# Token rows of 2112 bytes instead of 2056 in a sliding-window attention and expert-routing kernel

## The chip, the core and the metric

The kernel runs on one core of one Trainium2 chip. The metric is the device time of one execution in microseconds (us). TensorE (PE in the profile, PEld for its weight loads) multiplies matrices, VectorE (DVE) and ScalarE (ACT) do elementwise work, GpSimd (POOL) builds constants and issues the indirect transfers, and SyncE (SP) issues the plain transfers between memory and the core's on-chip memory of 128 partitions.

## What is computed

The first half is causal attention over a window of 128 positions, for 8 sequences of 576 tokens with 8 heads of 64 values. The second half is a mixture of experts without dropped tokens: each of the 4608 tokens (rows of 512 values) goes to the one of 8 experts with the largest gate logit.

```python
rel = pos[:, None] - pos[None, :]
scores = scale * q @ k.T - slope[h] * abs(rel)      # where 0 <= rel < 128, else -1e9
x = softmax(scores) @ v                             # (8, 8, 576, 64) -> (4608, 512)
logits = x @ w_gate                                 # 8 experts
e = argmax(logits, axis=1)
y = maximum(x @ w1[e], 0) @ w2[e]                   # 512 -> 1024 -> 512, by expert
out = softmax(logits)[e] * y
```

All values are float32.

## The kernel before, in words

**Attention and routing (about 0 to 226 us).** The work goes in units `u` of one sequence and one pair of heads, 32 in all. In each turn of the loop over `u`, `load_qk` and `load_v` ask SyncE for data some turns ahead, `scores(u)` does 36 small matmuls (L639) whose exponentials ScalarE takes (L646), `values(u - 1)` multiplies by v (L672), and `factors(u)` on VectorE applies the position factors and the mask (L652, L657). When a sequence is complete, its routing is spread over the turns that follow: logits, the chosen expert, and the place of each token in that expert's region of a table in memory (`pick`, `place`, which leave row numbers in `slots`). The order of the instructions on each engine is the order in which this code is written out (`manual_schedule`); no planner moves them.

**The token rows.** The table `x_rows` in memory has one region of 4608 rows for each expert. A row is `RW` values: the 512 values of the token, its number as an integer, and one over the sum of its gate exponentials. With `RW = Dm + 2` that is 514 values, 2056 bytes. `row` writes the 512 values for two tiles of 128 tokens into a buffer `xs` (L807, VectorE). The two trailing values lie ready in a small tile `ends`: the token numbers are put in once (L603), the gate weights by sequence (L791). `send` lets GpSimd copy them behind the row (L820), and `scatter` then issues an indirect transfer of 128 rows from `xs` into `x_rows` (L135). There are 36 such scatters. Slots of a region that hold no token are filled with `zero_row`, also by indirect transfers from L135 (`clear`), whose token number is out of range so that the result is dropped later.

**The hand-over.** Expert 0 has its first 256 rows read early: `early_group` clears what is unused of them, reads them back (L851), and `last_tasks` runs their first layer between the last pieces of routing. SyncE's read of the next rows of expert 0 (L1151) can only be issued when the last scatter and the last clear have landed.

**Experts (226 us on).** For each expert a group of 4 tiles of 128 rows, then a group of one tile for what lies above 512 rows. `gather` reads the group's rows into `xg` (L1151), `turn` transposes them on TensorE (L497), `tokens` copies the two trailing values out (L485, L486), the layers are matmuls of 256 columns in a seven-product scheme (L1048) or plain ones (L506, L517), and `send_out` scatters the results to the output by token number (L465). The weights of the next groups and the rows of the next groups are loaded while a group is computed. SyncE runs its loads in the order of the code, each when its buffer is free.

**On-chip memory.** Tiles are placed one behind the other in pools, each rounded up to 32 bytes per partition. The pools `consts` and `rte` lie first, so a change of size in them moves all tiles behind. `tab` is a pool of the attention stage alone, and its space is used again by the experts. The function `shifted` is a second, slower form of the attention for inputs whose sums leave a safe range; it stands in the program, and none of its lines has an instruction in the trace.

Of the kernel before, what the change touches and what calls it, by code (L numbers as in the profile page):

```python
# [8 lines left out]
F32 = mybir.dt.float32  # L9
# [6 lines left out]
P = 128  # L16
# [5 lines left out]
def kernel(  # L22
# [12 lines left out]
    nc = tc.nc  # L35

    Dm, N = qT.shape
# [3 lines left out]
    NT = N // P  # L41
# [19 lines left out]
    rte = ctx.enter_context(tc.tile_pool(name="rte", bufs=1))  # L61
# [50 lines left out]
    lmin = rte.tile([P, NT], F32, name="lmin")  # L112


    RW = Dm + 2
    x_d = nc.dram_tensor("x_rows", (E * N, RW), F32, kind="Internal").ap()
    zero_row = consts.tile([P, RW], F32, name="zero_row")
    soon.append(lambda: nc.gpsimd.memset(zero_row[:], 0.0))
# [25 lines left out]
    def clear(rows, apart=True):  # L144
        for j in range(rows.shape[1]):
            to_x_rows(zero_row[:], rows[:, j : j + 1], apart)
# [65 lines left out]
    def number_all_free(tmp_pool):  # L212

        tmp = tmp_pool.tile([P, E, NJ], F32, name="free", bufs=1)
        late = tmp_pool.tile([P, 1], F32, name="late", bufs=1)
        nc.vector.tensor_scalar_max(late[:], cnt[:, 0:1], float(EJ * P))
        number_free(
            late_free[:], tmp[:, 0, :EJ], late[:].to_broadcast([P, EJ]), tail[:, :EJ],
            region[:, 0:1].to_broadcast([P, EJ]), CAP,
        )  # L220
        number_free(
            free_rows[:], tmp[:], cnt[:].unsqueeze(2).to_broadcast([P, E, NJ]),
            tail[:, None, :].to_broadcast([P, E, NJ]), region[:].unsqueeze(2).to_broadcast([P, E, NJ]), CAP,
        )

    def scatter(t, row):
        to_x_rows(row, slots[:, t : t + 1])
# [26 lines left out]
    def shifted():  # L254
        with tc.tile_pool(name="bias", bufs=1) as b_pool, \
# [44 lines left out]
            for t in range(NT):  # L300
# [77 lines left out]
                gw = rows.tile([P, 1], F32, name="gw")  # L378
                nc.scalar.activation(gex[:], lgn[:, t, :], AF.Exp, bias=lmin[:, t : t + 1], scale=-1.0, accum_out=gw[:])
                nc.vector.tensor_scalar_add(gw[:], gw[:], 1e-9)  # L380
                if t == NT - 1:
                    number_all_free(rows)
                xs = rows.tile([P, RW], F32, name="xs")
                nc.scalar.copy(xs[:, :Dm], xf)
                nc.vector.tensor_copy(xs.bitcast(I32)[:, Dm : Dm + 1], tok_i[:, t : t + 1])
                nc.vector.reciprocal(xs[:, Dm + 1 :], gw[:])
                scatter(t, xs[:])


# [163 lines left out]
    with tc.tile_pool(name="tab", bufs=1) as tab, \  # L553
# [45 lines left out]
        rs_all = rte.tile([P, NT, H], F32, name="rs_all")  # L599
        gsum = rte.tile([P, NT], F32, name="gsum")  # L600

        ends = rte.tile([P, NT, 2], F32, name="ends")
        later.append(lambda: nc.vector.tensor_copy(ends.bitcast(I32)[:, :, 0], tok_i[:]))  # L603
        q_sb, k_sb, v_sb, xT, lT = {}, {}, {}, {}, {}
        probs, exps, sums = {}, {}, {}
# [190 lines left out]
        def row(ts, i):  # L796
            t = ts[i]
            pair, c = t // TP, t % TP * P
            if i % RG == 0:
                xs_of[t] = rows.tile([P, RG, RW], F32, name="xs", bufs=3)  # L800
            xs = xs_of[t] = xs_of[ts[i // RG * RG]]
# [46 lines left out]
        def early_group():  # L848
            clear(early_free, False)
            g = dict(n=EJ, apart=True, xg=plain.tile([P, EJ, RW], F32, name="xg2"))  # L850
            nc.sync.dma_start(g["xg"][:], x_d[: EJ * P, :].rearrange("(j p) r -> p j r", p=P))  # L851
# [292 lines left out]
    def gather(g):  # L1144
        n = g["n"]
        if g.get("e", 0) > 0:
            clear(free_rows[:, g["e"], :])
        xg = g["xg"] = pools["x"].tile([P, NJ, RW], F32, name="xg")
        src = g["rows"]().rearrange("(j p) r -> p j r", p=P)
# [120 lines left out]
    with nothing.Else():  # L1270
        n_bad = nc.values_load(n_more_i[0:1, 1:2], min_val=0, max_val=N * H)
        with tc.If(n_bad > 0):
            n_pass[0] = 1
            shifted()
            clear(free_rows[:, 0, :])
            with moe_pools(), tc.manual_schedule():
                experts(False)

        n_short = nc.values_load(n_more_i[0:1, 3:4], min_val=0, max_val=EJ * P)
        with tc.If(n_short > 0):  # L1280
            with moe_pools():
                plain_group(dict(n=EJ, e=0, rows=lambda: x_d[: EJ * P, :], apart=False))

        nx = nc.values_load(n_more_i[0:1, 0:1], min_val=0, max_val=NX)
        with tc.If(nx > XU):
            with moe_pools(), tc.For_i(XU, nx, 1) as i:
                mk = pools["u"].tile([P, 2, 1], I32, name="mk")
                nc.vector.tensor_copy(mk[:], xmasks[:, :, bass.ds(i, 1)])
                x = bass.ds(i, 1)
                plain_group(dict(n=1, x=x, rows=lambda: rows_of_x(x), mask=mk, apart=False))  # L1290
# [29 lines left out]
```

## Time and profile before

| what | us |
|---|---|
| three runs | 723.05, 723.74, 725.93 (median 723.74) |
| span of the profiled execution | 722.1 |
| TensorE busy in the span | 689.2 (95%) |
| VectorE, ScalarE, GpSimd busy | 345.5, 215.5, 120.2 |
| moved between memory and core | 121.49 MB, 168 GB/s over the span |
| one indirect transfer of rows on GpSimd | about 1.0, of 107 |

An engine that is busy nearly all the time leaves little to win by anything that other engines or transfers do. So the questions to the profile are where TensorE is idle, what ends each of these idle stretches, and whether one of them hangs on a token row.

### The profile page before, as it was taken

Reading aid. Unit: us, or ns where it says so; the run is one execution under the profiler, and the core shown is the slowest. Engines: PE = TensorE matmul, PEld = TensorE weight load, DVE = VectorE, ACT = ScalarE, POOL = GpSimd, SP = SyncE. Lnnn points to the kernel's source line nnn. Section 1 sums busy time; section 2 is a strip of 40 time slices with the busy share of each in tenths; the row PEclk is TensorE's granted clock in tenths of the full one; section 3 lists DMA queues with packets and bytes.
Section 4 is the critical chain, followed back from the end, with each engine's and each line's share of the span. In section 5 each row is a group of like instructions: output and inputs, shape, how many; then the busy total and the mean of one; then the engine's idle time right before and its main releaser. Section 6 shows DMA issues by size and latency. Waiting matters only on the chain.

```text
span 722.1 us, 13669 instructions
## 1 busy us (share of the span) xinstructions
PE 689.2 (95%) x5662; PEld 560.0 (78%) x5662; DVE 345.5 (48%) x705; ACT 215.5 (30%) x543; POOL 120.2 (17%) x146
## 2 busy tenths in 40 slices
PE   6999999999899999999999999999999999999991
PEld 5777676776676678878897887889788888978880
DVE  4577566575763354326335533634462463435300
ACT  6655454554411121122131212112121221212120
POOL 1010322023443020121022002202200220200020
PEclk9999999899999999999999999999999999999996
DMA  9976799852226726265353617534352835371010
GB/s 275 270 213 188 238 259 296 229 175 75 90 86 215 268 89 232 64 234 175 132 183 141 236 58 284 188 133 161 143 192 115 283 120 201 99 271 53 1 60 4
DMA packets 52722, 121.49 MB, mean 168 GB/s; under 512 B 7185, under 2 KB 7185, under 8 KB 52656
## 3 DMA queue, kind: packets, MB, share of 16 engines
q1 hardware_dynamic: 43568, 101.50, 43.7%
q0 software_dynamic: 8560, 19.06, 7.1%
q8 instruction: 45, 0.74, 0.4%
q14 instruction: 21, 0.17, 0.1%
q10 hardware_dynamic: 528, 0.02, 0.0%
HBM read 101.51 MB, written 28.12 MB: 180 GB/s over the span
## 4 chain that ended last, share of the span: by engine, by line
PE 82%; issue 11%; DVE 3%; POOL 1%; DMA 1%; ACT 0%; SPq 0%; POOLq 0%; DVEq 0%
PE b L1048 17%; PE a L1048 11%; PE c L1048 11%; PE m L672 7%; PE sp L639 7%; PE a L517 6%; PE sm L693 3%; PE b L506 3%; PE a L506 3%; PE m L804 2%; PE m L506 2%; PE c L506 2%; PE tp L497 1%; PE m L753 1%; PE c L517 1%
## 5 line engine op out<-in xcount | busy, mean ns | idle before, releaser
L465 POOL DMA_INDIRECT out_dram<-zo,si x28 | 29.7, 1060 | 292.8 <-ACT zo L1118 288.5
L646 ACT ACTIVATE e<-sp 128x384 f32<-128x384 f32 x128 | 55.8, 491 | 51.8 <-PE sp L639 30.8
L672 PE MATMUL m<-probs,v_sb 64*64 64x192 f32 (+2 forms) x1152 | 64.4, 315 | 6.6 <-issue 4.8
L672 PEld LDWEIGHTS m<-probs,v_sb 64*64 64x64 f32 x1152 | 52.7, 135 | 18.4 <-issue 10.8
L639 PE MATMUL sp<-q_sb,k_sb 64*64 64x192 f32 (+2 forms) x1152 | 57.9, 326 | 7.1 <-DMA k_sb<-in_kT_dram 5.2
L639 PEld LDWEIGHTS sp<-q_sb,k_sb 64*64 64x64 f32 x1152 | 47.5, 139 | 18.4 <-issue 12.9
L517 PE MATMUL a<-w,h 128*128 128x512 f32 x128 | 56.3, 592 | 0.0
L1118 ACT ACTIVATE zo<-zo,gw 128x256 f32<-128x256 f32 x42 | 19.1, 501 | 119.4 <-DVE zo L1129 78.2
L1048 PE MATMUL a<-xgT,w 128*128 128x256 f32 x224 | 53.0, 379 | 0.0
L1048 PE MATMUL b<-xTs,w1s 128*128 128x256 f32 x224 | 52.9, 379 | 0.0
L1048 PE MATMUL a<-w,h_sb 128*128 128x256 f32 x224 | 50.6, 379 | 0.0
L1048 PE MATMUL b<-w2s,hs 128*128 128x256 f32 x224 | 50.6, 379 | 0.0
L1048 PEld LDWEIGHTS a<-xgT,w 128*128 128x128 f32 x224 | 42.5, 190 | 8.7 <-issue 3.3
L1048 PEld LDWEIGHTS b<-xTs,w1s 128*128 128x128 f32 x224 | 42.6, 190 | 5.8
L1048 PEld LDWEIGHTS b<-w2s,hs 128*128 128x128 f32 x224 | 42.6, 190 | 5.8
L1048 PEld LDWEIGHTS a<-w,h_sb 128*128 128x128 f32 x224 | 42.0, 190 | 5.4
L652 DVE TENSOR_TENSOR probs<-e,fac 128x1152 f32<-128x1152 f32 x32 | 43.2, 1351 | 2.8 <-ACT e L646 2.8
L517 PEld LDWEIGHTS a<-w,h 128*128 128x128 f32 x128 | 23.7, 190 | 26.8 <-issue 26.8
L135 POOL DMA_INDIRECT x_rows<-xs,slots x36 | 37.9, 1053 | 15.1 <-POOL xs L820 6.4
L1078 DVE TENSOR_TENSOR u<-b,p 128x512 f32<-128x512 f32 x14 | 9.7, 692 | 56.7 <-PE b L1048 28.8
L681 DVE TENSOR_TENSOR xT<-xT,m 128x128 f32<-128x128 f32 x32 | 9.1, 283 | 52.5 <-ACT xT L680 51.2
L1082 ACT ACTIVATE h_sb<-h_sb 128x512 f32<-128x512 f32 x14 | 8.8, 630 | 84.3 <-DVE h_sb L1081 84.3
(246 smaller groups left out, 1152.2 us busy)
## 6 DMA issues: line engine op xcount, KB each, us to landing
w<-in_moe_w_dram SPq DMA_DIRECT2D x28, 2048.0 KB
q_sb<-in_qT_dram SPq DMA_DIRECT2D x32, 288.0 KB
k_sb<-in_kT_dram SPq DMA_DIRECT2D x32, 288.0 KB
xg<-x_rows SPq DMA_DIRECT2D x16, 514.0 KB
v_sb<-in_v_dram SPq DMA_DIRECT2D x24, 256.0 KB
w<-in_moe_w_dram SPq DMA_DIRECT2D x8, 512.0 KB
v_sb<-in_v_dram SPq DMA_DIRECT2D x24, 128.0 KB
xg<-x_rows SPq DMA_DIRECT2D x7, 257.0 KB
```

Of the source, the lines that this page charges most:

```text
L135: ins = nc.gpsimd.indirect_dma_start(out=x_d[:, :], out_offset=bass.IndirectOffsetOnAxis(ap=numbers, axis=0), in_=row, in_offset=None, bou ...
L465: ins = nc.gpsimd.indirect_dma_start(out=out[:, :], out_offset=bass.IndirectOffsetOnAxis(ap=g["si"][:, j : j + 1], axis=0), in_=row, in_of ...
L506: nc.tensor.matmul(ps[:, :n], lhsT=g["w1"][:, db, fb * P : (fb + 1) * P], rhs=g["xT"][:, db, :n], start=(db == 0), stop=(db == DB - 1),)
L517: nc.tensor.matmul(ps[:], lhsT=g["h"][:, fb, j * P : (j + 1) * P], rhs=g["w2"][:, fb, :], start=(fb == 0), stop=(fb == FB - 1),)
L639: nc.tensor.matmul(sp_banks[2 * par + s][r * HALF : (r + 1) * HALF, c : c + n], lhsT=k_sb[u][head, k0 : k0 + HALF], rhs=q_sb[u][head, q0 : ...
L646: nc.scalar.activation(exps[u][:, c], sp_banks[s][:, : W // 2], AF.Exp, scale=D ** -0.5)
L652: nc.vector.tensor_tensor(to[:, :, : 3 * C].rearrange("p a (j c) -> p a j c", c=C), e[:, :, : 3 * C].rearrange("p a (j c) -> p a j c", c=C ...
L672: nc.tensor.matmul(xp[r][par * HALF : (par + 1) * HALF, q0 : q0 + n], lhsT=v_sb[b][keys, i, h * D : (h + 1) * D], rhs=probs[u][keys, par, ...
L693: nc.tensor.matmul(sm[g : g + 32, i * HALF : i * HALF + C], lhsT=one_c[:, hp, :], rhs=probs[u][:, par, c : c + C], start=(hp == 0 and i == ...
L804: nc.tensor.transpose(m[:, 2 * hp : 2 * hp + 2, :].rearrange("p h d -> p (h d)"), xT[pair][:, hp, c : c + P], ident[:],)
L1048: nc.tensor.matmul(out_of[:, i, :], lhsT=lhs(i, k), rhs=rhs(k), start=(first and i == 0 and k == 0), stop=(k == nk - 1), skip_group_check= ...
L1118: nc.scalar.activation(o[:, th, dh, i, :], src[:, i, :], AF.Copy, scale=g["gw"][:, j : j + 1])
```

## The change

A row gets 528 values: the 512, the token number, the gate weight and 14 zeros, 2112 bytes, which is 33 times 64. Every row of the table then begins and ends at a multiple of 64 bytes. What follows from it: `zero_row`, `xs`, `xg` and the early group's `xg` become 56 bytes longer per row; `ends` holds 16 values per token tile instead of 2, is cleared once by GpSimd, and moves from the pool `rte` to the pool `tab`; GpSimd's copy at L820 moves 16 values per row instead of 2; and in `shifted` each `xs` is cleared behind the 512 values before it is filled.

```diff
-    RW = Dm + 2
+    RE = 16
+    RW = Dm + RE
     x_d = nc.dram_tensor("x_rows", (E * N, RW), F32, kind="Internal").ap()
     zero_row = consts.tile([P, RW], F32, name="zero_row")
...
                 xs = rows.tile([P, RW], F32, name="xs")
+                nc.vector.memset(xs[:, Dm:], 0.0)
                 nc.scalar.copy(xs[:, :Dm], xf)
                 nc.vector.tensor_copy(xs.bitcast(I32)[:, Dm : Dm + 1], tok_i[:, t : t + 1])
-                nc.vector.reciprocal(xs[:, Dm + 1 :], gw[:])
+                nc.vector.reciprocal(xs[:, Dm + 1 : Dm + 2], gw[:])
                 scatter(t, xs[:])
...
-        ends = rte.tile([P, NT, 2], F32, name="ends")
+        ends = tab.tile([P, NT, RE], F32, name="ends")
+        nc.gpsimd.memset(ends[:], 0.0)
         later.append(lambda: nc.vector.tensor_copy(ends.bitcast(I32)[:, :, 0], tok_i[:]))
```

## The prediction

> **What bounds the kernel now.** I read the totals first, then busy time by stage, then what TensorE waits for.
>
> ```profile
> span 722.1 us, 13669 instructions
> PE 689.2 (95%) x5662; PEld 560.0 (78%) x5662; DVE 345.5 (48%) x705; ACT 215.5 (30%) x543; POOL 120.2 (17%) x146
> ```
>
> TensorE is idle for 722.1 - 689.2 = 32.9 us in all. By stage (from the first matmul to the last attention work, the experts, the end):
>
> ```profile
> 5.00:226.00 221.00, 208.69 (x3295) 157.30 (x3296) 138.45 (x393) 107.58 (x314) 51.87 (x66) 0.98 0.67 198
> 226.00:631.00 405.00, 405.00 (x1994) 341.02 (x1993) 180.05 (x269) 89.99 (x191) 58.50 (x56) 1.00 0.49 171
> 631.00:722.00 91.00, 75.54 (x377) 61.70 (x376) 24.26 (x38) 16.56 (x37) 6.84 (x7) 0.94 0.22 81
> ```
>
> After the window and its length, the first figure is TensorE's busy time. In the experts' stage it is 405.00 of 405.00 us, although all but one of the reads of token rows fall there or just ahead of it. 5 us are lost before the first loads land, 15.5 at the end, where the last outputs land and the program closes, and 12.3 in attention and routing. What ends those 12.3 (us in total, times, longest):
>
> ```profile
> PE m L672 <- issue: 4.8, 18, 0.8
> PE m L506 <- DVE gw L486: 1.6, 1, 1.6
> PE sp L639 <- issue: 1.5, 5, 0.5
> PE m L672 <- DVE xs L807: 0.8, 2, 0.5
> ```
>
> No wait of a matmul here names a token-row transfer. One weight load does, for 0.3 us, in TensorE's order of time around the hand-over (start, length, work, idle before it):
>
> ```profile
> 191.40 1.09 PE L497 MATMUL sp<-ident,xg 128*128 128x128 f32 x8
> 192.33 0.71 PE L771 MATMUL m<-ident,lT 128*128 128x128 f32 x5
> 194.65 3.69 PE L506 MATMUL m<-xT,w 128*128 128x256 f32 x16 [1.61 <-DVE gw L486]
> ...
> 224.19 1.04 PE L497 MATMUL tp<-ident,xg 128*128 128x128 f32 x8
> ```
>
> The reads that feed the two L497 rows were issued by SyncE at:
>
> ```profile
> 186.93 0.38 SPq L851 DMA_DIRECT2D xg<-x_rows  x1
> 214.56 0.39 SPq L1151 DMA_DIRECT2D xg<-x_rows  x1
> ```
>
> The second read's data packets end at 218.1 us by the trace's transfer records, 6.1 us before TensorE takes them. That is the slack of the whole chain of scatters, clears and reads at the hand-over.
>
> [...] a packet of one 2056-byte row read has a median of 85 ns, one of 2048 bytes 84 ns; a scatter's packet of two rows, 4112 bytes, 169 ns against 159 for 4096. At most 9 ns of 169 are there to win.
>
> [...] A row of 2056 bytes shifts the next one by 8, a row of 2112 doesn't. Here the trace shows no price: VectorE writes `xs` at both kinds of offsets, and its 36 instructions lie within 6% (row below); the transposes of `xg` from all four offsets take 272 to 273 ns.
>
> [...]
>
> **The change part by part.** In the built program the executed instructions and waits of all five engines stand in the same order as before; GpSimd has one more, the clearing of `ends`. The 36 added clears of VectorE lie in `shifted`, which isn't run: 0 us.
>
> *Longer transfers.* 39 tiles read and 36 scattered, times 128 rows times 56 bytes, is 0.54 MB on 121.49, or 0.44%. Each read grows by 56/2056 = 2.7%. The early read's packets take some 2.6 us, so it lands at most 0.07 us later; its weight load then waits 0.37 instead of 0.3 us. But TensorE stands 1.61 us before 194.65 for VectorE, whose chain from 191.50 to 194.65 runs without a gap on other work and takes the early rows only at 193.87, against a transpose that ends at 192.5. So the 0.07 is hidden. The second read: 0.07 against 6.1 us. The others: behind a TensorE that never stands.
>
> *GpSimd.* Relevant rows:
>
> ```profile
> L807 DVE TENSOR_TENSOR xs<-m,rs_all x36: 650/682/694, 43.1 to 207.9; 128x512 f32<-128x512 f32 x36
> L135 POOL DMA_INDIRECT x_rows<-xs,slots x36: 975/984/1655, 50.5 to 209.4; - x36
> L820 POOL COPY xs<-ends x20: 187/199/214, 49.6 to 207.7; 128x4 int32<-128x4 int32 x16, 128x2 int32<-128x2 int32 x4
> ```
>
> The numbers after x20 are the least, median and greatest duration in ns. The copy of 4 elements becomes one of 32. The clear of `zero_row` took 527 ns for 514 elements and 190 for one, 0.66 ns an element, so the copy grows by 0.02 us; doubled, because it reads as well, 0.04. Twenty of them are 0.4 to 0.8 us on an engine that is busy 17%; the three of the last sequence add 0.06 to 0.12 us to the chain that has 6.1 us of slack. The clear of 576 elements takes 0.53 x 576/514 = 0.59 us near 3 us. GpSimd's constants then end at 4.6 instead of 4.0; the first is read at 11.05 (L86), and `ident` at 32.3 (L714). [...] Bounds 0 and 0.59, both hidden.
>
> *Issue of scatters.* One of 2056-byte rows takes 984 ns, one of the output's 2048-byte rows 977 (L465). I take no change; the upper bound, a doubling, is a rival below.
>
> *Moved addresses.* The built program puts `q_sb`, `k_sb`, `v_sb` and the second weight pool 32 bytes past a multiple of 64 before, and on multiples of 256 after. The first weight pool is on multiples of 256 already, so two 2 MB loads show what this is worth; speed in 40 slices of 506.9 to 513.6 us (first pool) and of 539.6 to 546.0 (second):
>
> ```profile
> GB/s 24 196 220 73 0 147 73 220 342 440 391 416 465 318 465 465 367 391 391 391 465 391 416 416 440 440 440 416 416 440 416 391 440 416 416 342 49 49 0 0
> ...
> GB/s 0 128 77 154 51 0 102 282 307 102 333 307 384 410 333 410 435 410 358 384 410 410 410 486 410 410 410 435 435 410 486 435 461 410 410 410 435 410 359 321
> ```
>
> Both settle near 415 GB/s, and a 4096-byte packet has a median of 159 ns in both. Value: 0.
>
> The sum is 0, with bounds of -0.3 (the early read's wait gone) and +1.3 us (0.07 + 0.12 + 0.59 + 0.4, were none of it hidden). 723.7 + 0 = **723.7 us**.
>
> **The rivals.**
>
> *The aligned rows and tiles relieve the attention stage, 719.2 us.* The transfer engines are 67% busy from 5 to 226 us and 94% in the first 20. The 4.8 + 1.5 us of TensorE idle there that end in "issue", where the profile sees no releaser, could be transfers that it can't name, those of instructions included (16 KB each, about 1 us). If two thirds of 6.3 and the 0.3 of the early read go, that is 4.5 us. Against it: the two weight loads[...].
>
> *The scatters get dearer, 728.0 us.* A two-row packet grows from 4112 to 4224 bytes. If GpSimd then needed twice the time to issue one, the 7 issues from 202.6 us on (5 scatters, 2 clears) would add 7 us, 0.9 more than the slack, and with the landing some 1.2 us in all; and buffers `xs` freed later would double the waits behind VectorE's row and routing work in attention (TensorE's and its weight loads' on L807, L773 and L196: 2.0 + 0.8 + 2.1 = 4.9 at most, of which I count 3.1, since weight loads partly lie beside matmuls). Against it: [...] row length doesn't show in the issue time.
>
> *Extra work on the path unhidden, 725.0 us*: the +1.3 above. It counts as no change.
>
> **How the numbers follow.** No change that a measurement tells: 0.74 (0.66 for my forecast, 0.08 for the unhidden work). Faster relief: 0.15. Dearer scatters: 0.11. The bounds of the costs alone give 723.4 to 725.0; the three earlier runs spread from 723.05 to 725.93. To leave out no more than 2 in 10 the range reaches most of the way to both outer rivals: 720.0 to 727.0.
>
> **What would show it.** Right: L135 stays near 984 ns, L820 grows to 220 to 240, TensorE's 226 to 631 us window stays full, the weight load before the 191.4 us transposes waits 0.3 to 0.4, and "issue" before L672 stays near 4.8. Wrong: a much smaller or larger "issue" sum in attention, or L135 well over 1 us. What would break the forecast is a dependence on addresses that no instruction of this trace shows, because nearly all its tiles share one offset.

## The result, and the profile after

The changed kernel takes 720.19 us (median of 4 runs, 719.94 to 721.9) against 724.73 us for the kernel before in the runs beside it: a ratio of 0.9942 with a 95% interval of 0.9914 to 0.9971. That is inside the forecast's range, 0.19 us above its lower end. But it is 0.58% faster, at an interval that leaves out 1, where the forecast said no change. The totals, and busy time by stage (the same windows as for the kernel before; each engine's busy time with its count, then the granted clock of TensorE, the share of the transfer engines, and GB/s):

```profile
span 718.6 us, 13672 instructions
PE 685.5 (95%) x5662; PEld 558.3 (78%) x5662; DVE 345.9 (48%) x705; ACT 214.8 (30%) x543; POOL 121.9 (17%) x147
```

```profile
5.00:226.00 221.00, 208.45 (x3309) 158.21 (x3310) 139.08 (x397) 107.86 (x316) 53.65 (x67) 1.00 0.65 205
226.00:631.00 405.00, 405.00 (x2011) 341.82 (x2010) 179.85 (x266) 90.04 (x193) 58.47 (x55) 1.00 0.49 172
```

The experts' window is full again. What TensorE waited for, and the row work (least, median and greatest duration in ns after the count):

```profile
PE m L676 <- issue: 5.2, 19, 1.1
PE m L509 <- DVE gw L489: 1.4, 1, 1.4
PE m L676 <- DVE xs L811: 0.8, 2, 0.5
```

```profile
L811 DVE TENSOR_TENSOR xs<-m,rs_all x36: 650/684/692, 43.0 to 204.5; 128x512 f32<-128x512 f32 x36
L137 POOL DMA_INDIRECT x_rows<-xs,slots x36: 976/987/1478, 50.4 to 206.0; - x36
L824 POOL COPY xs<-ends x20: 211/218/232, 49.5 to 204.2; 128x32 int32<-128x32 int32 x16, 128x16 int32<-128x16 int32 x4
```

The scatter's issue time (984 ns before, 987 after) and the copy (199, now 218) are as priced. The "issue" sum before the probabilities' product (L672, now L676) did not shrink: 4.8 before, 5.2 after. Yet the span is 3.5 us shorter. Setting the start of every matmul of one trace against the same matmul of the other shows where: within 0.65 us of each other up to 122.5 us (but for short stretches, in which they come up to 2.9 apart), 3.3 to 4.1 apart by 132 us, and from 196 us on a constant 3.45 us. The windows around that place, first of the kernel before, then of the changed one:

```profile
20.00:122.00 102.00, 97.62 (x1822) 75.58 (x1814) 68.93 (x176) 56.51 (x166) 16.96 (x23) 1.00 0.83 239
122.00:135.00 13.00, 11.25 (x137) 7.57 (x140) 5.41 (x19) 3.59 (x10) 4.02 (x6) 0.74 1.03 286
```

```profile
20.00:122.00 102.00, 97.69 (x1819) 75.98 (x1815) 68.97 (x176) 55.80 (x164) 17.72 (x23) 1.00 0.80 246
122.00:135.00 13.00, 11.92 (x200) 8.55 (x200) 7.55 (x24) 6.53 (x22) 3.92 (x6) 1.00 0.92 302
```

In 13 us TensorE did 137 matmuls before and 200 after, because its granted clock was 0.74 on average before and 1.00 after. The clock record has it at one half for 6.83 us from 126.99 us on. It fell behind a row of pauses of TensorE. This is the timeline of the kernel before at that place (start, length, work, idle before it):

```profile
124.00 0.55 PE L639 MATMUL sp<-q_sb,k_sb 64*64 64x64 f32 x4 [0.25 <-issue]
124.73 0.41 PE L639 MATMUL sp<-q_sb,k_sb 64*64 64x128 f32 x2 [0.17 <-issue]
125.45 0.21 PE L639 MATMUL sp<-q_sb,k_sb 64*64 64x64 f32 x1 [0.31 <-issue]
126.18 0.21 PE L639 MATMUL sp<-q_sb,k_sb 64*64 64x64 f32 x1 [0.52 <-issue]
```

Every 0.73 us or so, about half a microsecond passes from one start to the next, where 0.06 is the mean (1822 matmuls in the 102 us before). Such groups stand at 54 to 56, 77 to 81, 101 to 103, 123 to 128, 150 to 152 and 174 to 177 us in this trace, in the stretches in which scatters of token rows are issued and land, and the changed kernel has them too; the group near 124 us is only shorter there, and no fall of the clock follows. Every fall recorded inside the work, in every kernel with scatters, lasts 3.41 or 6.83 us, at 0.50.

So in this pair of traces the 3.5 us arise at one fall of the clock. But is that the cause, or what happened in these two executions? Two theories came first. *Clock*: the change makes pauses, and with them falls of the clock, rarer. *Addresses and rows*: aligned tiles and rows make the transfers of the attention stage shorter, and what waits for them waits less. The second had this behind it: the mean transfer record of a 2304-byte packet (a row of `q_sb` or `k_sb`) between 20 and 226 us was 128.7 ns before and 118.0 after, with a median of 93 in both. The quicker half of the packets is the same; it is the slow ones that got shorter (the slowest tenth begins at 175 ns before and at 154 after).

### The profile page after: what moved, and what is told of

It is laid out like the page before. It is cut to its first block, busy times and chain, and to the rows that moved or that the text cites. A ratio compares the mean times of both kernels' runs of the same rounds, so it can differ in the third digit from the quotient of the medians.

```text
span 718.6 us, 13672 instructions
## 1 busy us (share of the span) xinstructions
PE 685.5 (95%) x5662; PEld 558.3 (78%) x5662; DVE 345.9 (48%) x705; ACT 214.8 (30%) x543; POOL 121.9 (17%) x147
## 4 chain that ended last, share of the span: by engine, by line
PE 81%; issue 11%; DVE 4%; POOL 1%; DMA 1%; ACT 0%; SPq 0%; POOLq 0%; DVEq 0%
PE b L1052 17%; PE a L1052 12%; PE c L1052 12%; PE m L676 7%; PE sp L643 6%; PE a L520 6%; PE sm L697 3%; PE b L509 3%; PE a L509 3%; PE m L808 2%; PE m L509 2%; PE c L509 2%; DVE probs L656 1%; PE tp L500 1%; PE m L757 1%
## 5 line engine op out<-in xcount | busy, mean ns | idle before, releaser
L676 PE MATMUL m<-probs,v_sb 64*64 64x192 f32 (+2 forms) x1152 | 63.8, 310 | 7.4 <-issue 5.2
L676 PEld LDWEIGHTS m<-probs,v_sb 64*64 64x64 f32 x1152 | 52.2, 132 | 19.7 <-issue 12.2
L643 PE MATMUL sp<-q_sb,k_sb 64*64 64x192 f32 (+2 forms) x1152 | 55.4, 320 | 6.1 <-DMA k_sb<-in_kT_dram 5.3
L656 DVE TENSOR_TENSOR probs<-e,fac 128x1152 f32<-128x1152 f32 x32 | 43.3, 1352 | 2.5 <-ACT e L650 2.5
L137 POOL DMA_INDIRECT x_rows<-xs,slots x36 | 38.2, 1061 | 14.7 <-POOL xs L824 6.7
```

What stands on the lines that cost most here:

```text
L137: ins = nc.gpsimd.indirect_dma_start(out=x_d[:, :], out_offset=bass.IndirectOffsetOnAxis(ap=numbers, axis=0), in_=row, in_offset=None, bou ...
L643: nc.tensor.matmul(sp_banks[2 * par + s][r * HALF : (r + 1) * HALF, c : c + n], lhsT=k_sb[u][head, k0 : k0 + HALF], rhs=q_sb[u][head, q0 : ...
L656: nc.vector.tensor_tensor(to[:, :, : 3 * C].rearrange("p a (j c) -> p a j c", c=C), e[:, :, : 3 * C].rearrange("p a (j c) -> p a j c", c=C ...
L676: nc.tensor.matmul(xp[r][par * HALF : (par + 1) * HALF, q0 : q0 + n], lhsT=v_sb[b][keys, i, h * D : (h + 1) * D], rhs=probs[u][keys, par, ...
```

## The experiments

Twelve runs on three chips, each beside the kernel before on the same chip. Times are medians. "q, k" is the mean of a 2304-byte load packet between 20 and 226 us; "v" is the mean of a 2048-byte load packet before 175 us (5632 of them, 4608 of which are rows of `v_sb`; the others bring weights). "Tiles" is where `q_sb`, `k_sb`, `v_sb` and their neighbours begin, modulo 256.

```
chip  kernel         tiles  rows      us      ratio [95% interval]      q, k ns   v ns
A     before again   160    2056     721.54  1.0010 [0.9987, 1.0034]   129.6     122.4
A     after again    0      2112     718.82  0.9948 [0.9928, 0.9968]   119.0     117.8
A     addr_only      0      2056     719.37  0.9963 [0.9945, 0.9981]   124.2     120.6
A     rows_only      160    2112     720.74  0.9981 [0.9964, 0.9997]   120.8     124.0
B     spread         0      2112     706.17  0.9940 [0.9919, 0.9961]   121.0     115.6
B     off64          64     2112     709.00  0.9973 [0.9951, 0.9996]   126.0     123.5
B     rows_2304      192    2304     709.84  0.9995 [0.9969, 1.0021]   122.9     125.0
C     after third    0      2112     706.28  0.9961 [0.9941, 0.9982]   118.6     115.1
C     spread again   0      2112     706.25  0.9956 [0.9935, 0.9977]   120.3     111.6
C     pad_only       0      2056     706.81  0.9970 [0.9947, 0.9993]   124.8     117.2
C     off64 again    64     2112     709.05  0.9999 [0.9977, 1.0021]   122.8     124.3
```

The kernel before took 722.29 us on chip A, 710.91 on B and 709.09 on C; on B and C it was timed, and no trace of it was kept. The twelfth run, without scatters, is told below.

**The kernel before and the changed one again**, without any edit, on chip A.

> The kernel before, unchanged, to have the granted clock and a second trace beside its times. The trace of before shows half clock for 6.83 us at 127 us, the trace after shows none; up to 122 us the two run within 0.2 us of each other, and by 134 us the changed kernel is 3.9 us ahead. Theory clock: nearly every run of the kernel before falls to half clock once in attention, so 723 to 726 us, and its second trace again shows such an episode behind a group of pauses of TensorE. Rival (transfers alone, clock by accident): about half of the runs have no episode and lie near 720.3, and the difference to the changed kernel goes away.

> The changed kernel, unchanged, for more runs. Theory clock: most runs without an episode, 719.9 to 720.4 us, at a granted clock of 0.991 to 0.993; the few with one near 722 at 0.986. Rival (accident): as many episodes as in the kernel before, and a median within 1 us of it.

The ratio was 1.001 for the first and 0.9948 for the second: the gain is real, and repeats. The clock is no full account of it. The two new traces have one fall of 3.41 us each, at 126.57 and at 81.73 us. Over the runs of the two kernels, span x 2 x (1 - mean granted clock) gives 16.2 us at half clock for the kernel before and 13.5 for the changed one (13 to 15 of that is the idle end of a program). Over all kernels of chip A, a microsecond more at half clock goes with 0.41 us more of span. So 2.7 us less would be 1.1 of the 3.1 us between the two mean spans; 2 us are something else.

**Addresses alone.** The tiles keep the changed kernel's sizes and places, but rows of 514 values at a pitch of 2056 bytes go to memory and back:

```diff
-    x_d = nc.dram_tensor("x_rows", (E * N, RW), F32, kind="Internal").ap()
+    MW = Dm + 2
+    x_d = nc.dram_tensor("x_rows", (E * N, MW), F32, kind="Internal").ap()
...
-            in_=row, in_offset=None, ...
+            in_=row[:, :MW], in_offset=None, ...
...
-            nc.sync.dma_start(xg[:, j0:j1, :], src[:, j0:j1, :])
+            nc.sync.dma_start(xg[:, j0:j1, :MW], src[:, j0:j1, :])
```

> The changed kernel with rows of 514 values and a pitch of 2056 bytes in memory, as before; all tiles on the chip where the changed kernel has them (loads of q, k and v on multiples of 256 bytes). Theory addresses (loads to aligned tiles take less of the transfer engines, so TensorE's pauses get fewer): near 720.2 us, as after. Theory rows (aligned rows make the scatters lighter): 723 to 726, as before. Theory timing (any shift decides whether pauses add up to an episode): anything between, not ordered by either.

**Rows alone.** The changed kernel with 160 bytes of padding, which moves the attention tiles back to the place modulo 256 that they had before:

```diff
     plain = ctx.enter_context(tc.tile_pool(name="plain", bufs=1))
+    pad = plain.tile([P, 40], F32, name="pad")
```

> The changed kernel with rows of 528 values at 2112 bytes, and 160 bytes of padding that put the tiles for q, k, v and all behind them 160 past a multiple of 256, where they are before. Theory rows: near 720.2 us, as after. Theory addresses: 723 to 726, as before. Theory timing: anything between.

Addresses alone came to 0.9963, where the changed kernel has 0.9948. Rows alone came to 0.9981, at an interval that all but touches no change; with the tiles moved as well, the changed kernel takes 0.9973 of that (0.9962 to 0.9989, by resampling the single runs).

**Without scatters.** The scatters go to a row number past the table's end, which is meant to keep them from writing, and eight plain transfers fill the table with zeros from 142 us on (this kernel's tiles begin at 32 modulo 256):

```diff
-        to_x_rows(row, slots[:, t : t + 1])
+        to_x_rows(row, nowhere[:])
...
```

> The changed kernel with the scatters of token rows sent to a row number beyond the table, so that they move no row; the part of the table that is read is filled with zero rows by eight plain transfers from about 160 us on, and the experts work on zeros and write no output. Only the attention stage up to 150 us is read. Theory scatters (TensorE's groups of pauses of about 0.5 us near 54, 78, 101, 124 and 150 us, and with them the fall to half clock, come from the scatters' transfers): these groups are gone, no half clock before 150 us, and the work that stands at 145 us in the changed kernel stands 5 to 9 us earlier. Rival (the routing work that comes in the same turns, or the supply of instructions): the groups stay and the work is less than 2 us earlier.

729.5 us in one run; the total says nothing here, since the table is filled until 175 us, ahead of the hand-over, and the clock falls there for 17.07 us. Up to 150 us, though, TensorE has no group of pauses. That looked like proof that the scatters make them, and it isn't: it ran on chip B, and *no* trace on chips B or C has such groups, scatters or not. The kernels are 11 to 13 us faster there than on chip A, about what the 18 to 24 pauses of half a microsecond in each of its traces cost. What makes the pauses, and why chip A has them and the others don't, stays open.

**Scatters less bunched.** At most one in a turn of attention:

```diff
-            for _ in range(min(len(unsent), 3 if len(unsent) > 6 else 2)):
+            for _ in range(min(len(unsent), 2 if len(unsent) > 4 else 1)):
```

> The changed kernel with at most one scatter in a turn of the attention loop (two while more than four wait) instead of two or three. Theory scatters: as many pauses, but no more than two together, so that no stretch is idle enough for half clock in attention: the shares of the clock that the runs list go to 0.992 or 0.993 in nearly all, and the time to 1 us or more below the changed kernel. Rival (pauses come with the routing work): groups of pauses and the time as in the changed kernel, within 0.5 us.

**Tiles 64 bytes off.** The changed kernel with `pad = plain.tile([P, 16], ...)`: the attention tiles come to 64 modulo 256; the first weight pool stays on multiples of 256.

> The changed kernel with 64 bytes of padding, so that the tiles behind it lie 64 past a multiple of 256 instead of on it, the second row of a pair and all loads included. If a multiple of 64 is enough: as the changed kernel, 0.995 of before. If loads gain from multiples of 256 only: as the kernel with aligned rows alone, 0.998 of before, and loads of 2304 bytes in attention at 121 ns on average instead of 118.

**Rows of 2304 bytes**, a multiple of 256. The scatter writes 2304, the reads take 2112. Three fixed `xs` tiles, whose pad is cleared once, take the place of rotating ones; the tiles of attention come to 192 modulo 256:

```diff
+    MW = 576
...
-    x_d = nc.dram_tensor("x_rows", (E * N, RW), F32, kind="Internal").ap()
+    x_d = nc.dram_tensor("x_rows", (E * N, MW), F32, kind="Internal").ap()
...
-            nc.sync.dma_start(xg[:, j0:j1, :], src[:, j0:j1, :])
+            nc.sync.dma_start(xg[:, j0:j1, :], src[:, j0:j1, :RW])
```

> The changed kernel with rows of 2304 bytes at that pitch in memory, so that each begins at a multiple of 256; reads take 2112 bytes of each, scatters write 2304, 9% more than in the changed kernel; tiles lie 192 past a multiple of 256. If the beginning at 256 counts for the scatters: 0.5 to 1.5 us below the changed kernel. If bytes count: 0.5 to 1.5 us above it. If 64 is enough and bytes are hidden: within 0.5 us.

0.9995 for the best aligned rows of all (with tiles at 192 and 9% more bytes written), 0.9973 for tiles at 64, and 0.994 with spread scatters. The last had no unaltered changed kernel beside it on chip B. So the open points were put on one chip, C.

**The changed kernel, and padding alone.** The second of these is the *kernel before* with one line, and with nothing of the change proper:

```diff
     plain = ctx.enter_context(tc.tile_pool(name="plain", bufs=1))
+    pad = plain.tile([P, 24], F32, name="pad")
```

> The changed kernel a third time, to stand beside the next three on one chip. Theory addresses and rows: a ratio of 0.994 to 0.995 as twice before, on any chip, since load packets get shorter whether or not TensorE pauses. Theory clock: if the change helped by making pauses and falls of the clock rarer, it helps less on a chip without the groups of 0.5 us pauses: 0.997 to 1.000 there.

> The kernel before with 96 bytes of padding ahead of the attention tiles and nothing else: q_sb, k_sb, v_sb, e, probs and xT at multiples of 256 as after, rows, copies and transfers of token rows as before. Theory addresses: ratio about 0.996, load packets of q and k near 124 ns (118 to 119 in the changed kernel, 129 in the one before). Theory rows: 0.999 to 1.000, packets near 129. Theory accident (any shift in timing moves the time by some tenths of a per cent): anything between 0.994 and 1.003.

**Spread and 64 bytes off, beside them.**

> The changed kernel with at most one scatter in a turn, two while more than four wait. Theory that bunched scatters cost time: 0.2 to 0.4% less than the changed kernel of the same call, and single runs that differ by half as much. If it is equal to the changed kernel, the 0.994 of its first run was the change's own.

> The changed kernel with the attention tiles 64 bytes past a multiple of 256. If a multiple of 64 is all that matters: equal to the changed kernel of the same call within 0.1%, packets near 119 ns. If 256 matters: 0.2 to 0.4% slower than it, packets of q and k near 126 ns, as in the first run of this kernel.

Resampling the single runs gives intervals for ratios on this chip. Padding alone (0.9970 against before) isn't to be told from the changed kernel, whose ratio to it is 0.9993, 0.9972 to 1.0009. Tiles at 64 cost 1.0039, 1.0025 to 1.0053, against the changed kernel, and leave nothing of the gain. (On chip B, against the kernel with spread scatters, they cost as much, 1.0040, 1.0024 to 1.0055, though 0.27% against the kernel before is left there.) Spreading the scatters is 1.0000, 0.9987 to 1.0012: that theory falls, and the 0.994 on chip B was the change's own. No version beats the changed kernel.

It is the place of the tiles modulo 256 that counts, then: 0 gains, and of 64, 160 and 192, the others that were tried, none gains as much. An accident of any shift is unlikely: the six entries with tiles at 0, come by in four ways, gained 0.30 to 0.60%, and the four others 0.01 to 0.27%. Which tiles matter isn't separated: the padding moves those that the loads write together with `e`, `probs` and `xT`, which the engines write. The load packets speak for the loads. Those of 2048 bytes follow the tiles on every chip, 111.6 to 120.6 ns at 0 and 122.4 to 126.3 elsewhere (with the kernel without scatters). The mean of the 2304-byte ones alone would mislead: 120.8 at 160 on chip A, and on chip C 122.8 at 64, less than the 124.8 of padding alone.

**Where on the path it counts.** On chip C, without groups of pauses, it can be read. From 226 us on, the starts of all matmuls of the four kernels run at constant distances from one another (none moves by over 0.01 us): all that differs arises before. What TensorE waited for between 30 and 165 us, in the changed kernel and then with tiles at 64 (whose lines are numbered one higher):

```profile
PE m L676 <- DVE xs L811: 0.8, 2, 0.5
PE m L194 <- DVE pre L182: 0.7, 3, 0.3
PE m L676 <- DVE sc L198: 0.5, 1, 0.5
```

```profile
PE m L809 <- issue: 1.4, 1, 1.4
PE m L194 <- DVE pre L182: 0.7, 3, 0.3
PE sp L644 <- issue: 0.7, 1, 0.7
PE m L677 <- DVE xs L812: 0.5, 1, 0.5
PE m L677 <- issue: 0.5, 1, 0.5
```

Three single waits for "issue", 2.6 us, that the changed kernel doesn't have. One of them in the timeline of the kernel with tiles at 64:

```profile
128.76 0.55 PE L809 MATMUL m<-ident,xT 128*128 128x128 f32 x3
...
130.66 0.53 PEld L809 LDWEIGHTS m<-ident,xT 128*128 128x128 f32 x5 [1.59 <-issue]
130.66 0.77 PE L809 MATMUL m<-ident,xT 128*128 128x128 f32 x5 [1.36 <-issue]
```

It stops in the middle of a run of eight equal transposes, and the profile shows no wait for data there. One line of the page offers a reason:

```profile
q8 instruction: 45, 0.74, 0.4%
```

45 packets of 16 KB. TensorE has 11,458 records in the changed kernel's trace, 254.6 for each packet; by an estimate from that, a packet holds 256 of its instructions. So these look like its own instructions, and the profile lists them among the packets of the transfer engines, beside the loads. Counting its records, the three stops, and one at 23 us, come before numbers 705, 4033, 4546 and 4802: that is 193, 193, 194 and 194 past a multiple of 256, the same place in a packet each time. The packets' ends are at 23.58, 108.67, 120.86 and 129.32 us, and TensorE goes on at 24.95, 110.06, 122.40 and 130.66: 1.34 to 1.54 us later each time. That fits packets that come too late. In the experts, where 256 instructions last 19 to 32 us, packets end some 22 us or more ahead of that place and no such stop is seen; in attention 256 instructions last 5.5 to 8.4 us on this chip.

Late packets are not long ones: these four took 1.04 to 1.21 us, the others before 192 us 0.89 to 1.48. They start late. In all fourteen traces a packet starts, at the earliest, when TensorE is at place 152 or 153 of the 256 before. Counted from place 152, packets start 0.7 to 1.1 us later where the transfer engines move nothing (on chips B and C at about 150 us), and the late ones of these chips 4.8 to 8.6 us later, in stretches in which the transfer engines are 97% busy or more. The kernel without scatters tries this out, though it wasn't made for it. It fills the table where the others load next to nothing, and the three packets there start 4.4, 5.5 and 6.4 us after that place, against 0.7 to 1.8 us in the seven other traces of chips B and C; one of them stops TensorE, for 0.47 us.

The waits of this kind before 192 us (stops at that place, with their whole length from one matmul's start to the next), one trace each, with the time of the very run that was traced, the mean of all runs, and the time that the 13,824 load packets of 2304 and 2048 bytes before 175 us took, shared among 16 engines:

```
chip  kernel         tiles   late instructions, us   this run   mean us   load packets, us
C     after third    0        1.3                     706.33     706.58    100.4
C     spread again   0        1.5                     706.61     706.58    100.0
B     spread         0        1.5                     706.14     706.41    101.8
C     pad_only       0        2.8                     705.66     707.20    103.9
C     off64 again    64       5.4                     707.92     709.02    105.4
B     off64          64       5.8                     711.62     708.80    106.9
B     rows_2304      192      6.5                     709.24     710.16    105.8
```

Late instructions, mean time and load packets go together: from the first row to the last, 5.2 us more of stops, 3.6 us more of mean time and 5.4 us more of load packets. Run by run it is looser: the traced run with padding alone was the fastest of the seven. On chip C the changed kernel is 4.4 us ahead of tiles at 64 at 165 us, of which 4.1 are these stops, and 1.5 us ahead from 180 us on. The rest is given back at the hand-over, where TensorE waits for the early read of token rows, first in the changed kernel, then with tiles at 64:

```profile
PE sp L500 <- DMA xg<-x_rows: 3.3, 1, 3.3
PE sp L501 <- DMA xg<-x_rows: 2.7, 1, 2.7
```

Being early, the changed kernel waits 0.6 us longer. The larger part is the clock: in its trace it falls to one half for 6.83 us from 171.82 us on, behind that wait, and in the other there is no fall there. The single runs of the changed kernel also scatter less (standard deviation 1.3 us, against 2.2 with padding alone and with tiles at 64); since padding alone has its tiles at 0 too, this account doesn't explain it.

On chip A and in the first pair this account isn't shown. There the groups of pauses hold TensorE back by 10 to 13 us, so TensorE reaches that place some 5 us after the packet's end in the median, against about 3 on C, and the stops sum to 2.2 us before, 1.9 after, 1.0 in the kernel before again and 2.4 in the changed one again. The gain there (0.52%, 0.58%) is as large; clock falls make about a third of it, by the estimate above; the rest isn't assigned. On B and C the link from crowded transfers to late instructions has the kernel without scatters behind it. That the tiles' place makes the loads lighter, and so the packets of instructions timely, rests on load packets and late instructions going together; no run moved the loads of attention alone. And for want of a trace, the late instructions of the kernel before on these chips aren't known.

## Why the range held and the argument did not, point by point

720.19 us lies in the range of 720.0 to 727.0 by luck: the lower end was put that low for the sake of a rival, and on chip A the changed kernel's median was 718.82. Most of the signs named for the forecast came too (L137 at 987 ns, the experts' window full, "issue" before the probabilities' product at 5.2 us), and the time fell all the same: they don't tell the two cases apart.

*What bounds the kernel* held. The experts' window stayed at 405.00 of 405.00, and in the traces every difference arose before it.

*Longer transfers, GpSimd, issue of scatters* held, all at nothing that shows: 984 to 987 ns an issue, a two-row packet of 176.1 ns before and 175.7 after although it has 112 bytes more, the copy up by 19 ns on an engine that is 17% busy. The weight load for the early rows waited 0.6 us, not 0.3 to 0.4, and the next wait was 1.4 us instead of 1.6. That the added clear of `ends` can hold VectorE up by as much as its whole length, 0.59 us, was the author's estimate. The clear took 0.64 us. Beside it one VectorE instruction (L576, before L573) took 0.70 us instead of 0.36, the position factors began at 5.26 us instead of 4.90, ScalarE's wait behind them shrank from 0.90 to 0.65, and the first product on VectorE (L656, before L652) began at 9.41 instead of 9.30: 0.11 us, made up by 13.1 us. (The four terms of the upper bound, 0.07, 0.12, 0.59 and 0.4, make 1.2, not 1.3; nothing hangs on it.)

*Moved addresses. "Value: 0"* is the step that failed, and through it the sum. Moving the tiles alone is worth 0.30% (a line of padding, chip C) to 0.37% (the changed kernel with the old rows, chip A), 2.1 to 2.7 us. The evidence was of the wrong kind. The two weight loads run in the experts' stage with little beside them, and medians don't tell: the median 2304-byte packet is 93 ns at either address, before and after. What changed is the slow part of the loads in the crowded stage: all 13,824 load packets take 107.4 us of 16 engines before and 100.8 after (addresses alone 104.6, rows alone 104.9). It matters, by the traces of chips B and C, where the late ones of the packets that look like TensorE's instructions start 4.8 to 8.6 us after place 152, while the transfer engines are 97% busy or more.

*The rows: "At most 9 ns of 169 are there to win".* How much of that aligned rows win is neither shown nor ruled out: rows alone came to 0.9981, rows beside aligned tiles add 0.9992 (0.9978 to 1.0011, chip A) and 0.9993 (0.9972 to 1.0009, chip C), and rows at a multiple of 256, with tiles at 192, gained nothing. By the medians about 0.2% at most is theirs. Why tiles at 0 gain and tiles at 64, 160 and 192 little or nothing, no run shows.

*The rival "aligned rows and tiles relieve the attention stage, 719.2 us"* was right in direction, place and size: 720.19. It had also named what the traces of chips B and C point to, transfers that the profile can't name, "those of instructions included (16 KB each, about 1 us)". Its working wasn't right: it let two thirds of the 6.3 us of "issue" waits go, and in the pair of traces they went from 4.8 + 1.5 + 0.4 to 5.2 + 0.5 + 0.6 (the last of each before L693, now L697). Most of these were the groups of pauses, which the change leaves alone. The weight against it was the two loads of weights, judged above, and an estimate of the author's for the rows that no run shows.

*"What would break the forecast is a dependence on addresses that no instruction of this trace shows"* is what happened. A line of padding would have been its test.

## What to carry to other kernels

When a change moves tiles, compare where they begin modulo 256 (here 0 gained 0.30 to 0.60%, and 64, 160 and 192 gained 0.01 to 0.27%), and judge the price of a load by all load packets of the crowded stage together; medians, lone loads and the mean of one kind misled here. Try the move alone, by padding, before crediting the change that came with it. A wait for "issue" in the middle of a run of like instructions is worth counting: if it falls at the same place modulo 256 among the engine's records (here 193 or 194), shortly after a packet of instructions has landed (here 1.34 to 1.54 us), the engine may have been waiting for its own code behind your loads.

## What the runs showed of the hardware

Chips differ by more than the change does: the kernel before took 722.29, 710.91 and 709.09 us on three, and the slower one has groups of half-microsecond pauses of TensorE, every 0.73 us, that no trace of the other two has. A single pair of traces can put the whole difference on an event, here one 6.83 us fall of the clock, that other pairs don't repeat: on chip C it is the changed kernel's trace that has such a fall (6.83 us from 171.8 us on), and it is 0.39% faster all the same.
